# Layer hand-over in a DFT and attention kernel: transposes moved from after the last DFT stage into it, by four row tiles, with the small norm operations on GpSimd

## The chip, the cores and the metric

The kernel runs on one core of one Trainium2 chip. The metric is the time of one execution on the device in microseconds (us), the median of several executions. "Before" is the kernel before the change and "after" the kernel with it. Engines are named as the profile names them: PE is TensorE (matmuls and transposes), PEld its weight loads, DVE is VectorE, ACT is ScalarE, POOL is GpSimd. PSUM is the on-chip memory into which TensorE writes its results here, SBUF the one from which the engines take their inputs; the copies bring results from PSUM to SBUF. The granted clock is the share of full speed that the chip allowed TensorE, as the profile records it.

## The reference

The model alternates two layers twice, each on a layer-normed input with a residual. Layer A is a two-dimensional DFT filter. Layer B is attention by segments of 32 tokens with 8 memory tokens that are handed from segment to segment.

```python
def _A_ref(x, w_r, w_i):
    X = rfft2(x.astype(float32)) * (w_r + 1j * w_i)
    return irfft2(X, s=(S, D)).astype(bfloat16)

def _B_ref(x, mem0, Wq, Wk, Wv, Wo, seg_len):
    mem = mem0
    for s in range(n_seg):                       # 64 segments of 32 tokens
        h = concatenate([mem, x[:, s*seg_len:(s+1)*seg_len]], axis=1)
        q, k, v = h @ Wq, h @ Wk, h @ Wv         # ... 32 heads of 128
        p = softmax(where(mask, q @ k.T * scale, -1e9))
        o = (p @ v) @ Wo
        mem = o[:, :M]; outs.append(o[:, M:])    # ...

x = x + _A_ref(_layernorm(x), A_w_r, A_w_i)      # x: 1 x 2048 x 640
x = x + _B_ref(_layernorm(x), ...)
x = x + _A_ref(_layernorm(x), A_w_r, A_w_i)
x = x + _B_ref(_layernorm(x), ...)
```

What matters here is the seam from A to B. It occurs twice. Layer B multiplies with the *transposed* normed tokens (`hT`; 640 channels as 5 blocks of 128 partitions), and layer A ends with tokens on the partitions, in 16 row tiles of 128 tokens.

## The kernel before

The last DFT stage works through the 16 row tiles. For each tile it makes two products: `psg` (channel DFT, copied to SBUF by ScalarE) and, one tile later, `psy` (token DFT plus residual, copied by ScalarE into `x`). VectorE takes the statistics of every tile and normalises every pair of tiles. `add_u` sums each segment's tokens with a small matmul into `psu`.

```python
def _ln_apply(nc, pool, mv, xin, xout, nt, eps_t, on_dve=False):
    # ... Ln and Exp on ScalarE give r0, then four small operations on 2 columns:
    nc.vector.scalar_tensor_tensor(out=t, in0=mv[:, :nt, 1], scalar=LN_EPS, in1=r0, op0=ALU.add, op1=ALU.mult)
    nc.vector.tensor_tensor(out=t, in0=t, in1=r0, op=ALU.mult)
    nc.vector.tensor_scalar(out=t, in0=t, scalar1=-0.5, scalar2=1.5, op0=ALU.mult, op1=ALU.add)
    nc.vector.tensor_tensor(out=t, in0=t, in1=r0, op=ALU.mult)
    if on_dve:
        for t in range(nt):
            nc.vector.tensor_scalar(out=xout[:, t, :], in0=xin[:, t, :], scalar1=mv[:, t, 0:1], scalar2=rs[:, t:t + 1], op0=ALU.subtract, op1=ALU.mult)
    # ...

# the stage, in layer A's tokens():
for s0 in range(16 + 5):
    if s0 < 16:
        spectrum_d(s0)                    # 6 matmuls -> psg, ScalarE copy (L399)
    if 1 <= s0 <= 16:
        tokens(s0 - 1)                    # 6 matmuls -> psy, ScalarE copy into x, statistics
    if s0 >= 2 and s0 % 2 == 1 and s0 < 18:
        norm((s0 - 3) // 2)               # _ln_apply of two tiles into xna
    if handoff is not None:
        # ...
        if s0 >= 5:
            handoff.add_u(pp, xna[:, s0 - 5, :], s0 - 5)
if handoff is not None:
    handoff.finish(pp)                    # psu -> u
pp.release()
if handoff is not None:
    handoff.transpose_all(xna)
```

The hand-over stands after the stage. For each of the five channel blocks it makes 16 transposes into one PSUM tile and empties that by groups of 15 segments, in runs of 16 neighbouring keys:

```python
def transpose_all(self, xna):
    # ...
    for c in range(5):
        ps = pt.tile([128, 16, 128], BF16, name="pstr", tag="pstr")
        for s0 in range(16):
            nc.tensor.transpose(out=ps[:, s0, :], in_=xna[:, s0, c * 128:(c + 1) * 128], identity=ident[:])
        for g_ in range(4):
            b = st.kbase(g_ * GS)
            dst = hT[:, c, b:b + GS * SW].rearrange("p (w t) -> p w t", t=SW)[:, :, 1:SW].rearrange("p w (j s) -> p w j s", s=16)
            src = ps[:, :, 2 * GS * g_:2 * GS * (g_ + 1)].rearrange("p s (w j) -> p w j s", j=2)
            (nc.vector.tensor_copy if g_ % 2 == 0 else nc.scalar.copy)(out=dst, in_=src)
        # ... four small copies for the last four segments
```

After that layer B starts with `psvb` (160 matmuls of the first guess of the memories), then its long loop over heads.

## Time and profile before

| | before |
|---|---|
| time, median of 4 runs (range) | 1655.17 us (1654.39 to 1655.83) |
| window: first matmul of the last DFT stage to first `psvb`, layers 1 and 2 | 49.9 and 49.9 us |
| of it in layer 2: to the end of the last token matmul / from there to the end of the last norm / from there to `psvb` | 28.5 / 5.9 / 15.5 us |

I call the stretch from the first matmul of the last DFT stage to the first `psvb` matmul **the window**. It exists twice per execution.

TensorE is busy for 94% of the span, so a change of order can win time only where TensorE stands still. The windows view of before (busy us of each engine in each stretch, number of instructions, then the granted TensorE clock) shows where in layer 2 that is:

```profile
core 0: us, PE busy (x) PEld busy (x) DVE busy (x) ACT busy (x) POOL busy (x), PEclk, DMA share, GB/s
...
906.00:936.00 30.00, 28.68 (x257) 20.58 (x256) 24.03 (x82) 24.07 (x46) 1.46 (x2) 1.00 0.88 316
936.00:943.00 7.00, 2.15 (x30) 1.77 (x31) 4.73 (x28) 1.32 (x5) 0.00 (x0) 0.71 0.95 293
943.00:956.00 13.00, 7.33 (x77) 6.99 (x75) 7.66 (x20) 6.54 (x20) 0.00 (x0) 0.76 0.27 75
```

The stage itself (906 to 936) is limited by TensorE at full clock. The tail behind it (936 to 956) has TensorE busy for less than half. The timeline of TensorE in before (start, duration, what, and in brackets the idle time before it with its releaser) shows the pace and the waits:

```profile
919.55 1.00 PE L399 MATMUL psg<-A2gt_S,A2UT_S 128*128 128x321 bf16 x6
...
921.35 1.00 PE L399 MATMUL psg<-A2gt_S,A2UT_S 128*128 128x321 bf16 x6
...
937.28 0.68 PE L1191 MATMUL psu<-sel,A2tok_S 128*128 128x64 bf16 x10 [2.20 <-DVE A2tok_S L120]
940.51 0.81 PE L1191 MATMUL psu<-sel,A2tok_S 128*128 128x64 bf16 x10 [2.55 <-DVE A2tok_S L120]
...
942.50 4.37 PE L1206 MATMUL pstr<-ident,A2tok_S 128*128 128x128 bf16 x48
...
956.32 6.20 PE L1248 MATMUL psvb<-u,B2wv_S 128*128 128x64 bf16 x160 [3.49 <-DVE B2hT_S L1218]
```

One row tile costs 1.80 us (919.55 to 921.35), with no wait. All waits are in the tail. The view of the transposes' PSUM tile in before gives the price of one block copy (minimum/median/maximum in ns) and, under "its engine sat idle before it", how long copies waited for a copy of the other engine:

```profile
L1211 DVE COPY B2hT_S<-pstr x10: 647/652/658, 944.4 to 954.2; 128x480 bf16<-128x480 bf16 x10
L1211 ACT COPY B2hT_S<-pstr x10: 562/562/562, 945.2 to 954.8; 128x480 bf16<-128x480 bf16 x10
...
  DVE B2hT_S L1211: 6.7, 5
```

ScalarE's and VectorE's copies out of one PSUM tile take turns; in before ScalarE stands idle for 6.7 us ahead of such copies, in the tail.

### The profile page before, as it was taken

Reading aid. Unit: us, or ns where it says so; the run is one execution under the profiler, and the core shown is the slowest. Engines: PE = TensorE matmul, PEld = TensorE weight load, DVE = VectorE, ACT = ScalarE, POOL = GpSimd, SP = SyncE. Lnnn points to the kernel's source line nnn. Section 1 sums busy time; section 2 is a strip of 40 time slices with the busy share of each in tenths; the row PEclk is TensorE's granted clock in tenths of the full one; section 3 lists DMA queues with packets and bytes.
Section 4 is the critical chain, followed back from the end, with each engine's and each line's share of the span. In section 5 each row is a group of like instructions: output and inputs, shape, how many; then the busy total and the mean of one; then the engine's idle time right before and its main releaser. Section 6 shows DMA issues by size and latency. Waiting matters only on the chain. (4 is left out here: it accounts for less than half of the span.)

```text
span 1658.3 us, 36195 instructions
## 1 busy us (share of the span) xinstructions
PE 1563.1 (94%) x14240; PEld 1081.0 (65%) x14241; DVE 790.0 (48%) x2300; ACT 835.6 (50%) x2528; POOL 282.4 (17%) x206
## 2 busy tenths in 40 slices
PE   4887999999999999899988789999999999999998
PEld 2566666666666666677755666666666666666775
DVE  5772455555545554543356724545545454544110
ACT  5373566666666666511114636666666666663000
POOL 0810112121211111100026002121211111111000
PEclk9998999999999999999999899999999999999999
DMA  4472143434434343633302703434344343436241
GB/s 155 156 274 72 53 148 132 155 117 148 136 138 144 130 154 127 233 125 96 96 13 88 260 2 110 160 116 150 132 142 137 133 156 127 140 130 226 68 127 54
DMA packets 167873, 218.05 MB, mean 131 GB/s; under 512 B 7374, under 2 KB 141836, under 8 KB 159756
## 3 DMA queue, kind: packets, MB, share of 16 engines
q1 hardware_dynamic: 167084, 213.34, 38.5%
q8 instruction: 113, 1.85, 0.4%
q0 software_dynamic: 608, 2.30, 0.4%
q14 instruction: 68, 0.56, 0.1%
HBM read 170.52 MB, written 45.09 MB: 130 GB/s over the span
## 5 line engine op out<-in xcount | busy, mean ns | idle before, releaser
L846 PEld LDWEIGHTS <-bB_S 128*128 128x128 bf16 x3180 | 260.2, 97 | 185.9 <-issue 6.6
L990 DVE TENSOR_TENSOR bB_S<-pso,bB_S 128x480 bf16<-128x480 f32 (+1 forms) x320 | 189.4, 592 | 266.3 <-PE pso L981 249.4
L925 ACT ACTIVATE bB_S<-pss 128x269 bf16<-128x269 f32 (+5 forms) x576 | 213.3, 385 | 191.7 <-PE pss L922 177.2
L1140 PE MATMUL psx<-Wo_sb,bB_S 128*128 128x320 bf16 x2048 | 288.2, 299 | 3.9 <-DMA bB_S<-oTx_d 3.9
L1140 PEld LDWEIGHTS <-bB_S 128*128 128x128 bf16 x2048 | 197.2, 98 | 80.5 <-DMA bB_S<-oTx_d 4.6
L905 DVE CAST bB_S<-psk 128x495 bf16<-128x495 f32 (+3 forms) x320 | 191.3, 598 | 115.0 <-PE psk L846 84.8
L950 POOL TENSOR_TENSOR bB_S<-bB_S,bB_S 128x634 f32<-128x634 f32 x64 | 99.2, 1550 | 820.9 <-ACT bB_S L946 809.9
L926 DVE TENSOR_TENSOR bB_S<-bB_S,maskf 128x269 bf16<-128x269 bf16 (+5 forms) x576 | 162.9, 287 | 152.9 <-ACT bB_S L925 149.2
L914 ACT CAST bB_S<-psv 128x512 bf16<-128x512 f32 (+1 forms) x288 | 160.5, 557 | 83.8 <-PE psv L912 83.4
L890 ACT ACTIVATE bB_S<-psq 128x480 bf16<-128x480 f32 x300 | 152.5, 508 | 97.9 <-PE psq L846 97.9
L846 PE MATMUL psk<-B2hT_S,bB_S 128*128 128x495 bf16 (+3 forms) x800 | 165.0, 342 | 2.6 <-DVE bB_S L905 1.4
L846 PE MATMUL psk<-B1hT_S,bB_S 128*128 128x495 bf16 (+3 forms) x800 | 165.0, 342 | 1.7 <-DVE B1hT_S L1225 1.2
L912 PE MATMUL psv<-bB_S,B1hT_S 128*128 128x256 bf16 x1360 | 163.4, 272 | 0.2 <-DVE bB_S L905 0.2
L912 PE MATMUL psv<-bB_S,B2hT_S 128*128 128x256 bf16 x1360 | 163.4, 272 | 0.2 <-DVE bB_S L905 0.2
L922 PEld LDWEIGHTS <-bB_S 128*128 128x128 bf16 x1216 | 103.1, 98 | 90.1 <-issue 6.3
L846 PE MATMUL psq<-B2hT_S,bB_S 128*128 128x495 bf16 (+5 forms) x780 | 157.6, 336 | 0.1
L846 PE MATMUL psq<-B1hT_S,bB_S 128*128 128x495 bf16 (+5 forms) x780 | 157.5, 336 | 0.1
L922 PE MATMUL pss<-bB_S 128*128 128x132 bf16 (+8 forms) x1216 | 148.4, 216 | 3.0
L912 PEld LDWEIGHTS <-B1hT_S 128*128 128x128 bf16 x1360 | 128.7, 98 | 13.7 <-issue 0.3
L912 PEld LDWEIGHTS <-B2hT_S 128*128 128x128 bf16 x1360 | 128.6, 98 | 13.7 <-issue 0.3
L981 PE MATMUL pso<-bB_S,bB_S 128*128 128x132 bf16 (+8 forms) x1216 | 119.6, 216 | 0.0
L981 PEld LDWEIGHTS <-bB_S 128*128 128x128 bf16 x1216 | 91.2, 98 | 15.7 <-DVE oTmf L991 0.5
(225 smaller groups left out, 1555.1 us busy)
## 6 DMA issues: line engine op xcount, KB each, us to landing
bB_S<-Rd SPq DMA_DIRECT2D x62, 1059.5 KB
oTx_d<-bB_S SPq DMA_DIRECT2D x60, 512.0 KB
bB_S<-oTx_d SPq DMA_DIRECT2D x56, 512.0 KB
bB_S<-in_B_Wq_dram SPq DMA_DIRECT2D x32, 320.0 KB
bB_S<-in_B_Wk_dram SPq DMA_DIRECT2D x32, 320.0 KB
bB_S<-in_B_Wv_dram SPq DMA_DIRECT2D x32, 320.0 KB
bB_S<-oTx_d SPq DMA_DIRECT2D x14, 384.0 KB
Wo_sb<-in_B_Wo_dram SPq DMA_DIRECT2D x4, 1280.0 KB
```

The source lines that it names most:

```text
L846: nc.tensor.matmul(ps, lhsT=w[:, ch, hh * 128:(hh + 1) * 128], rhs=src[:, ch, lo:hi], start=(ch == 0), stop=(ch == 4))
L890: nc.scalar.mul(out=qv[:, :, 0:SEG], in_=x_view(ps, o, n)[:, :, 1:SW], mul=scale)
L905: nc.vector.tensor_copy(out=KTs[h % 2][:, lo:hi], in_=ps[:, 0:hi - lo])
L912: nc.tensor.matmul(ps[:, i * 256:(i + 1) * 256], lhsT=hT[:, ch, (t + i) * 128:(t + i + 1) * 128], rhs=w["Wv"][:, ch, :], start=(ch == 0), ...
L914: nc.scalar.copy(out=V[:, t:t + n, :].rearrange("p a b -> p (a b)"), in_=ps[:, 0:n * 256])
L922: nc.tensor.matmul(ps[:, off - o0:off - o0 + hi - lo], lhsT=KT[:, t * 128:(t + 1) * 128], rhs=QT[:, lo:hi], start=True, stop=True)
L925: nc.scalar.activation(out=E[:, 0:n], in_=ps[:, 0:n], func=ACTF.Exp)
L926: nc.vector.tensor_tensor(out=P[:, o0:o0 + n], in0=E[:, 0:n], in1=bs.mask[:, o0:o0 + n], op=ALU.mult)
L950: nc.gpsimd.tensor_tensor(out=accS, in0=accS, in1=sums_sb, op=ALU.add)
L981: nc.tensor.matmul(pso[:, lo - q0:hi - q0], lhsT=V[:, t, (h % 2) * 128:(h % 2 + 1) * 128], rhs=P[:, off:off + hi - lo], start=(i == 0), st ...
L990: nc.vector.tensor_tensor(out=oT.rearrange("p (r s j) -> p r s j", r=16, j=2)[:, :, s0:s0 + ns, :], in0=byclass(po), in1=rx, op=ALU.mult)
L1140: self.tc.nc.tensor.matmul(ps[:, 0:320], lhsT=lhs(h, k // 2), rhs=self.g["Wo_sb"][:, h, c0:c0 + 320], start=(h == 0), stop=(h == H - 1))
```

## The change

Its intent is to empty the tail. Every four row tiles, the transposes of those tiles stand inside the stage, by two channel blocks per iteration, and only the last four tiles are left for the tail. Because a copy then sees four row tiles and not sixteen, it writes runs of four keys. To let one copy cover all four groups of segments, they get an equal pitch in `hT`, which shifts its columns from 512 on by 7. `norm` is split: the small operations go to GpSimd (`inverse`), the scaling stays on VectorE (`_ln_scale`) and comes one iteration later. The diff, cut to its core:

```diff
+def _ln_inverse(nc, pool, mv, nt, eps_t, small):
+    # ... Ln, Exp on ScalarE as before, then the small operations on `small`;
+    # GpSimd: five operations in place of VectorE's four
+        def inverse(q):
+            rs[q], _ = _ln_inverse(nc, wk, mv[q], 2, g["eps"], nc.gpsimd if q < 7 else nc.vector)
...
-            for s0 in range(16 + 5):
-                if s0 < 16:
-                    spectrum_d(s0)
-                if 1 <= s0 <= 16:
-                    tokens(s0 - 1)
-                if s0 >= 2 and s0 % 2 == 1 and s0 < 18:
-                    norm((s0 - 3) // 2)
-                    ...
-                    if s0 >= 5:
-                        handoff.add_u(pp, xna[:, s0 - 5, :], s0 - 5)
+            for i in range(16 + 4):
+                if i < 16:
+                    spectrum_d(i)
+                    ...
+                    if i >= 7 and i < 19 and (i - 7) % 4 < 3:
+                        handoff.rows(pp, xna, (i - 7) // 4, (i - 7) % 4 * 2)
+                    for s0 in range(i - 5, min(i - 4, 14)) if i < 19 else (14, 15):
+                        if s0 >= 0:
+                            handoff.add_u(pp, xna[:, s0, :], s0)
+                if 1 <= i <= 16:
+                    tokens(i - 1)
+                if i >= 3 and i % 2 == 1 and i < 18:
+                    inverse((i - 3) // 2)
+                if i >= 4 and i % 2 == 0 and i < 19:
+                    norm((i - 4) // 2)
+            if handoff is not None:
+                handoff.finish(pp)
+                handoff.rows(pp, xna, 3, 0, big=True)
+                handoff.rows(pp, xna, 3, 4)
...
+    def hcol(self, k):
+        return k + (self.PRE if k >= 512 else 0)          # PRE is 7
...
+    def rows(self, pp, xna, q, c0, big=False):
+        c1 = min(5, c0 + (4 if big else 2))               # channel blocks c0 to c1 of row tiles 4q to 4q+3
+        # ... one PSUM tile: "pstr" (one buffer), or a big one for four channel blocks
+        for c in range(c0, c1):
+            for i in range(4):
+                nc.tensor.transpose(out=ps[:, c - c0, i, :], in_=xna[:, s0 + i, c * 128:(c + 1) * 128], identity=self.g["ident"][:])
+        for c in range(c0, c1):
+            v = grp[:, c, :, :]...                        # all four groups of 15 segments
+            (nc.vector.tensor_copy if c % 2 == 0 else nc.scalar.copy)(
+                out=v[:, :, :, :, s0:s0 + 4], in_=ps[:, c - c0, :, 0:120].rearrange("p s (g w j) -> p g w j s", g=4, j=2))
+        for j in range(2):                                # the last four segments
+            nc.scalar.copy(out=v[:, :, :, j, s0:s0 + 4], in_=ps[:, 0:c1 - c0, :, 120 + j:120 + 2 * n:2].rearrange("p c s w -> p c w s"))
```

More of the change, by code (lines that the diff above doesn't have):

```diff
@@ L105, in _ln_stats @@
     nc.vector.bn_aggr(out=mv[:, t, :], in_=st[:, t, :, :])
-def _ln_apply(nc, pool, mv, xin, xout, nt, eps_t, on_dve=False):
+def _ln_inverse(nc, pool, mv, nt, eps_t, small):
     rs = pool.tile([128, 4], FP32, name="lnrs", tag="lnrs")
@@ L113, in _ln_apply, with _ln_scale @@
     nc.scalar.activation(out=r0, in_=r0, func=ACTF.Exp, scale=-0.5)
-    nc.vector.scalar_tensor_tensor(out=t, in0=mv[:, :nt, 1], scalar=LN_EPS, in1=r0, op0=ALU.add, op1=ALU.mult)
-    nc.vector.tensor_tensor(out=t, in0=t, in1=r0, op=ALU.mult)
-    nc.vector.tensor_scalar(out=t, in0=t, scalar1=-0.5, scalar2=1.5, op0=ALU.mult, op1=ALU.add)
-    nc.vector.tensor_tensor(out=t, in0=t, in1=r0, op=ALU.mult)
+    if small is nc.vector:
+        small.scalar_tensor_tensor(out=t, in0=mv[:, :nt, 1], scalar=LN_EPS, in1=r0, op0=ALU.add, op1=ALU.mult)
+    else:
+        small.tensor_scalar_add(out=t, in0=mv[:, :nt, 1], scalar1=LN_EPS)
+        small.tensor_tensor(out=t, in0=t, in1=r0, op=ALU.mult)
+    small.tensor_tensor(out=t, in0=t, in1=r0, op=ALU.mult)
+    small.tensor_scalar(out=t, in0=t, scalar1=-0.5, scalar2=1.5, op0=ALU.mult, op1=ALU.add)
+    small.tensor_tensor(out=t, in0=t, in1=r0, op=ALU.mult)
+    return rs, nb
+def _ln_scale(nc, mv, rs, xin, xout, nt):
+    for t in range(nt):
+        nc.vector.tensor_scalar(out=xout[:, t, :], in0=xin[:, t, :], scalar1=mv[:, t, 0:1], scalar2=rs[:, t:t + 1], op0=ALU.subtract, op1=ALU.mult)
+def _ln_apply(nc, pool, mv, xin, xout, nt, eps_t, on_dve=False):
+    rs, nb = _ln_inverse(nc, pool, mv, nt, eps_t, nc.vector)
     if on_dve:
-        for t in range(nt):
-            nc.vector.tensor_scalar(out=xout[:, t, :], in0=xin[:, t, :], scalar1=mv[:, t, 0:1], scalar2=rs[:, t:t + 1], op0=ALU.subtract, op1=ALU.mult)
+        _ln_scale(nc, mv, rs, xin, xout, nt)
         return
@@ L128, in _ln_tiles @@
     st = pool.tile([128, 4, 2, nc.vector.BN_STATS_DIM], FP32, name="lnst", tag="lnst")
-    mv = pool.tile([128, 4, nc.vector.BN_AGGR_DIM], FP32, name="lnmv", tag="lnmv")
+    mv = pool.tile([128, 4, nc.vector.BN_AGGR_DIM], FP32, name="lnmv", tag="lnmv", bufs=3)
     return st, mv
-SLOT = dict(S1=20480, S2=10880, S3=12288, S4=10240, S5=12166, S6=11776)
+SLOT = dict(S1=20480, S2=10940, S3=12288, S4=10240, S5=12166, S6=11776)
 class _Cut:
@@ L417, in tokens @@
                 nc.sync.dma_start(out=xd[:, 2 * q:2 * q + 2, :], in_=x[:, 2 * q:2 * q + 2, :])
+        rs = {}
+        def inverse(q):
+            rs[q], _ = _ln_inverse(nc, wk, mv[q], 2, g["eps"], nc.gpsimd if q < 7 else nc.vector)
         def norm(q):
             xno = xna[:, 2 * q:2 * q + 2, :]
-            _ln_apply(nc, wk, mv[q], x[:, 2 * q:2 * q + 2, :], xno, 2, g["eps"], on_dve=True)
+            _ln_scale(nc, mv[q], rs[q], x[:, 2 * q:2 * q + 2, :], xno, 2)
             nc.sync.dma_start(out=xnd[:, 2 * q:2 * q + 2, :], in_=xno)
         with tc.manual_schedule(engines={nc.tensor.engine, nc.scalar.engine, nc.vector.engine}):
-            for s0 in range(16 + 5):
-                if s0 < 16:
-                    spectrum_d(s0)
-                if 1 <= s0 <= 16:
-                    tokens(s0 - 1)
-                if s0 >= 2 and s0 % 2 == 1 and s0 < 18:
-                    norm((s0 - 3) // 2)
-                if handoff is not None:
-                    if s0 < 10:
-                        handoff.wv_piece(s0)
-                    if s0 >= 5:
-                        handoff.add_u(pp, xna[:, s0 - 5, :], s0 - 5)
-        if handoff is not None:
-            handoff.finish(pp)
+            for i in range(16 + 4):
+                if i < 16:
+                    spectrum_d(i)
+                if handoff is not None:
+                    if i < 10:
+                        handoff.wv_piece(i)
+                    if i == 4:
+                        handoff.memory(pp)
+                    if i >= 7 and i < 19 and (i - 7) % 4 < 3:
[13 more added lines that the diff above has]
+                handoff.rows(pp, xna, 3, 4)
         pp.release()
-        if handoff is not None:
-            handoff.transpose_all(xna)
 H, DH, MEM, SEG, NSEG = 32, 128, 8, 32, 64
@@ L526, in __init__ @@
             qpos[b:b + SW] = np.concatenate([MEM + np.arange(SEG), [MEM - 1]])
+        self.hgap = [(self.hcol(a), self.hcol(b)) for a, b in ((502, 512), (1007, 1024), (1519, 1536), (2035, 2048))]
         self.q0 = [0] + [self.qbase(g * GS) for g in range(1, self.NG)] + [self.NQ]
@@ L844, in chain @@
         def chain(w, hh, ps, src, lo, hi):
+            if src is hT:
+                lo, hi = st.hcol(lo), st.hcol(lo) + hi - lo
             for ch in range(5):
@@ L861, in q_x @@
                 n = GS if g_ < NG - 1 else 3
-                b = st.kbase(g_ * GS)
+                b = st.hcol(st.kbase(g_ * GS))
                 ps = pj.tile([128, 512], FP32, name="psq", tag="pj")
@@ L911, in v_tiles @@
                 for ch in range(5):
-                    nc.tensor.matmul(ps[:, i * 256:(i + 1) * 256], lhsT=hT[:, ch, (t + i) * 128:(t + i + 1) * 128], rhs=w["Wv"][:, ch, :],
+                    nc.tensor.matmul(ps[:, i * 256:(i + 1) * 256], lhsT=hT[:, ch, st.hcol((t + i) * 128):st.hcol((t + i) * 128) + 128], rhs=w["Wv"][:, ch, :],
                                      start=(ch == 0), stop=(ch == 4))
@@ L1171, in begin @@
     def begin(self):
-        self.hT = self.ar.get("S2", f"{self.lname}hT").bf(5, self.st.NK)
-        for a, b in ((502, 512), (1007, 1024), (1519, 1536), (2035, 2048)):
+        self.hT = self.ar.get("S2", f"{self.lname}hT").bf(5, self.st.NK + 12)
+        for a, b in self.st.hgap:
             self.tc.nc.gpsimd.memset(self.hT[:, :, a:b], 0.0)
@@ L1192, in add_u @@
                              skip_group_check=True)
-    def transpose_all(self, xna):
-        nc, g, st, hT, tc = self.tc.nc, self.g, self.st, self.hT, self.tc
-        ident, SW, GS = g["ident"], st.SW, st.GS
-        with tc.tile_pool(name="bs_pt", bufs=3, space=PSUM) as pt, tc.tile_pool(name="bs_pm", bufs=1, space=PSUM) as pm:
-            psm = pm.tile([128, 5, MEM], BF16, name="psm0")
-            for c in range(5):
-                nc.tensor.transpose(out=psm[:, c, :], in_=self.m0[:, c * 128:(c + 1) * 128], identity=ident[:MEM, :MEM])
-            nc.vector.tensor_copy(out=hT[:, :, 0:MEM], in_=psm[:])
-            nc.vector.tensor_copy(out=self.gq[:, :, 0:1], in_=psm[:, :, MEM - 1:MEM])
-            for c in range(5):
-                ps = pt.tile([128, 16, 128], BF16, name="pstr", tag="pstr")
-                for s0 in range(16):
-                    nc.tensor.transpose(out=ps[:, s0, :], in_=xna[:, s0, c * 128:(c + 1) * 128], identity=ident[:])
-                for g_ in range(4):
-                    b = st.kbase(g_ * GS)
-                    dst = hT[:, c, b:b + GS * SW].rearrange("p (w t) -> p w t", t=SW)[:, :, 1:SW].rearrange("p w (j s) -> p w j s", s=16)
-                    src = ps[:, :, 2 * GS * g_:2 * GS * (g_ + 1)].rearrange("p s (w j) -> p w j s", j=2)
-                    (nc.vector.tensor_copy if g_ % 2 == 0 else nc.scalar.copy)(out=dst, in_=src)
-                b = st.kbase(4 * GS)
-                dst = hT[:, c, b:b + 3 * SW].rearrange("p (w t) -> p w t", t=SW)[:, :, 1:SW].rearrange("p w (j s) -> p w j s", s=16)
-                nc.vector.tensor_copy(out=dst, in_=ps[:, :, 120:126].rearrange("p s (w j) -> p w j s", j=2))
-                b = st.kbase(NSEG - 1) + 1
-                nc.scalar.copy(out=hT[:, c, b:b + 16], in_=ps[:, :, 126])
-                nc.scalar.copy(out=hT[:, c, b + 16:b + SEG - st.TAIL], in_=ps[:, 0:16 - st.TAIL, 127])
-                nc.vector.tensor_copy(out=hT[:, c, st.TAILK:st.TAILK + st.TAIL], in_=ps[:, 16 - st.TAIL:16, 127])
@@ new lines, in memory @@
+    def memory(self, pp):
+        nc = self.tc.nc
+        psm = pp.tile([128, 5, 128], BF16, name="psm0", tag="pstr")
+        for c in range(5):
+            nc.tensor.transpose(out=psm[:, c, 0:MEM], in_=self.m0[:, c * 128:(c + 1) * 128], identity=self.g["ident"][:MEM, :MEM])
+        nc.vector.tensor_copy(out=self.hT[:, :, 0:MEM], in_=psm[:, :, 0:MEM])
+        nc.vector.tensor_copy(out=self.gq[:, :, 0:1], in_=psm[:, :, MEM - 1:MEM])
+    def rows(self, pp, xna, q, c0, big=False):
+        nc, st, hT = self.tc.nc, self.st, self.hT
+        SW, GS, s0 = st.SW, st.GS, 4 * q
+        c1 = min(5, c0 + (4 if big else 2))
+        if big:
+            ps = pp.tile([128, 4, 4, 128], BF16, name="pstrb", tag="pg", bufs=3)
+        else:
+            ps = pp.tile([128, 2, 4, 128], BF16, name="pstr", tag="pstr")
+        n = 4 if q < 3 else 3
+        b = st.hcol(st.kbase(4 * GS))
+        win = hT[:, :, b:b + 4 * SW].rearrange("p c (w t) -> p c w t", t=SW)
+        grp = hT[:, :, st.PRE:st.PRE + 4 * 512].rearrange("p c (g k) -> p c g k", g=4)[:, :, :, 0:GS * SW]
+        for c in range(c0, c1):
+            for i in range(4):
+                nc.tensor.transpose(out=ps[:, c - c0, i, :], in_=xna[:, s0 + i, c * 128:(c + 1) * 128], identity=self.g["ident"][:])
+        for c in range(c0, c1):
+            v = grp[:, c, :, :].rearrange("p g (w t) -> p g w t", t=SW)[:, :, :, 1:SW].rearrange("p g w (j s) -> p g w j s", s=16)
+            (nc.vector.tensor_copy if c % 2 == 0 else nc.scalar.copy)(
+                out=v[:, :, :, :, s0:s0 + 4], in_=ps[:, c - c0, :, 0:120].rearrange("p s (g w j) -> p g w j s", g=4, j=2))
+        v = win[:, c0:c1, 0:n, 1:SW].rearrange("p c w (j s) -> p c w j s", s=16)
+        for j in range(2):
+            nc.scalar.copy(out=v[:, :, :, j, s0:s0 + 4], in_=ps[:, 0:c1 - c0, :, 120 + j:120 + 2 * n:2].rearrange("p c s w -> p c w s"))
+        if n == 3:
+            nc.scalar.copy(out=win[:, c0:c1, 3, 1 + s0:5 + s0], in_=ps[:, 0:c1 - c0, :, 126])
+            nc.scalar.copy(out=hT[:, c0:c1, st.hcol(st.TAILK):st.hcol(st.TAILK) + 4], in_=ps[:, 0:c1 - c0, :, 127])
@@ L1223, in scatter @@
             lo, hi = max(1, g_ * st.GS), min((g_ + 1) * st.GS, NSEG)
-            b = st.kbase(lo)
+            b = st.hcol(st.kbase(lo))
             nc.vector.tensor_copy(out=hT[:, :, b:b + (hi - lo - 1) * st.SW + 1:st.SW], in_=gq[:, :, lo:hi])
```

## The prediction

> **What bounds now.** TensorE: 94% busy, 41% of the span on the chain of waits. The change touches the last DFT stage and the transposes before layer B, twice per run (timeline: second 906 to 956 us).
>
> - Stage, 906.4 to 935: TensorE-bound, 1.80 us per row tile back to back (28.7 of 30 us busy, clock 1.00; ScalarE and VectorE 24 each).
> - Tail, 935 to 956.3: TensorE mostly waits. Last norm done 940.8; 80 transposes from 942.5; VectorE and ScalarE copies (652/562 ns, taking turns) until 956.2; then psvb starts. Clock 0.71 to 0.76.
> - First stage matmul to psvb: 49.9 us.
>
> **Removed from the tail.** 60 of 80 transposes and three quarters of the copies. After the last norm I expect 0.35 us psu, 20 transposes (1.5 us at low clock), then copies in turn c0 VectorE, c1 ScalarE, c2, c3 (4 x 0.65), eight small ScalarE copies (about 0.07 each): about 5.4 us against 15.5. Gain 10 us per layer.
>
> **Added inside the stage.** TensorE +3.4 us (60 x 56 ns, the trace's spacing at 128 columns); VectorE +9 copies x 0.6, minus 7 x 0.74 of small norm operations; ScalarE +6 copies x 0.46 and 18 small ones. As busy time it fits; the order does not:
>
> 1. psu and transposes now stand *before* the iteration's token matmuls, and norm moved half a pair later. So in every odd iteration TensorE waits: token matmuls end, x copy (0.2+0.7 us), statistics (1.05), the new norm's scale (0.4 to 0.8), against only 0.83 us of DFT matmuls to cover it. Stall about 1.7 us per pair. Before, slack was nearly two iterations.
> 2. ScalarE's block copy waits for VectorE's and precedes the x copy, which the next statistics await, which precede the next VectorE block copy. Loop: copy 0.7, copy+small 0.6, x copy 0.7, statistics 1.05, norm 0.7 every second: over 3 us against 2.2 of TensorE.
>
> Walking the queues in program order with these durations gives 45 us to the last token matmuls (before: 28.7 measured; the same walk 28.2), psvb at 55 to 56, or 58 if the clock sags to about 0.85 (it is 0.84 to 0.88 in the preceding spectrum stage). An estimate: net +6 to +8 us per layer, twice.
>
> GpSimd: the Trainium skill (GPSIMD Engine Reference, section 3.1) puts its two-input operations at about half VectorE's speed; from the trace's large ones (1.55 us for 634 columns) I estimate 0.3 us per small one. Below about 0.5 us they are off the chain.
>
> hT shifts 7 columns. The skill (SBUF, Operand start alignment) asks only element alignment; the trace agrees: q matmuls at odd columns take 372 ns, k ones from aligned columns 372. No effect elsewhere.
>
> **Predicted: 1668 us, 1652 to 1684 (8 in 10).** Faster by over 2%: 0.02; within 2%: 0.87; slower by over 2%: 0.11.
>
> **Right or wrong in the profile.** Stage to last token matmuls 40 to 50 us, with TensorE waiting on norm outputs before psu or transposes in odd iterations; ScalarE block copies waiting on VectorE ones; clock in the stage below 1.00; last norm to psvb 5 to 7 us; layer B's period unchanged.
>
> **What would make it wrong.** If the stage stays near 33 us (order harmless), about 1640. If small GpSimd operations take 0.7 us, norm waits for them: 4 to 8 us more per layer. If weight loads from the shifted hT slow (1360 psv matmuls per layer), far slower.

## More of the kernel before

Lines of the page of before. The first is the span, the second busy time per engine, then two groups of layer B's matmuls (busy us, mean ns of one | idle before them).

```profile
span 1658.3 us, 36195 instructions
...
PE 1563.1 (94%) x14240; PEld 1081.0 (65%) x14241; DVE 790.0 (48%) x2300; ACT 835.6 (50%) x2528; POOL 282.4 (17%) x206
...
L846 PE MATMUL psk<-B2hT_S,bB_S 128*128 128x495 bf16 (+3 forms) x800 | 165.0, 342 | 2.6 <-DVE bB_S L905 1.4
...
L846 PE MATMUL psq<-B2hT_S,bB_S 128*128 128x495 bf16 (+5 forms) x780 | 157.6, 336 | 0.1
```

## The result, and the profile after

After takes 1678.63 us (median of 4 runs, 1676.28 to 1681.61), before 1655.17 us. The ratio is 1.0143, with a 95% interval of 1.0125 to 1.016: 23.5 us or 1.4% more.

| | before | after |
|---|---|---|
| time, us | 1655.17 | 1678.63 |
| window, layers 1 and 2, us | 49.9, 49.9 | 60.3, 60.4 |
| layer 2: to the end of the last token matmul, us | 28.5 | 47.3 |
| then to the end of the last norm, us | 5.9 | 7.1 |
| then to `psvb`, us | 15.5 | 6.0 |

After the last norm 9.5 us were gained, about what was expected. But the stage took 18.8 us more, and the stretch from its end to the last norm 1.2 us more. The page of after, the same lines:

```profile
span 1676.5 us, 36233 instructions
...
PE 1566.0 (93%) x14240; PEld 1078.0 (64%) x14241; DVE 783.0 (47%) x2228; ACT 837.9 (50%) x2556; POOL 295.7 (18%) x276
...
L878 PE MATMUL psk<-B2hT_S,bB_S 128*128 128x495 bf16 (+3 forms) x800 | 165.6, 343 | 2.8 <-DVE bB_S L937 1.5
...
L878 PE MATMUL psq<-B2hT_S,bB_S 128*128 128x495 bf16 (+5 forms) x780 | 158.0, 336 | 0.1
```

Busy time per engine is almost as it was; nothing on this page tells where 18 us of span went. (The profiled execution of before took 1660.0 us and so 5 us more than its timed runs' median; its first window begins 2.3 us later than that of after. So the spans of the two pages differ by less than the times.) The windows view of after shows it:

```profile
core 0: us, PE busy (x) PEld busy (x) DVE busy (x) ACT busy (x) POOL busy (x), PEclk, DMA share, GB/s
...
940.00:946.00 6.00, 4.56 (x49) 3.28 (x47) 3.19 (x9) 3.39 (x9) 0.92 (x5) 1.00 0.28 109
946.00:952.00 6.00, 3.44 (x26) 2.20 (x24) 3.89 (x10) 3.02 (x9) 1.08 (x5) 0.85 0.20 78
...
964.00:970.00 6.00, 2.68 (x32) 2.40 (x33) 4.05 (x22) 1.19 (x6) 0.00 (x0) 0.50 1.04 308
```

In the middle of the stage TensorE is busy for 4.56 of 6 us (before: 28.68 of 30), and VectorE and ScalarE for little more than half. No engine is full: this is a chain of waits, not a lack of throughput. TensorE's timeline in after shows which:

```profile
940.17 1.00 PE L412 MATMUL psg<-A2gt_S,A2UT_S 128*128 128x321 bf16 x6
941.00 0.28 PE L1248 MATMUL pstr<-ident,A2tok_S 128*128 128x128 bf16 x2
942.59 0.81 PE L1248 MATMUL pstr<-ident,A2tok_S 128*128 128x128 bf16 x6 [1.31 <-DVE A2tok_S L127]
...
948.45 0.38 PE L1248 MATMUL pstr<-ident,A2tok_S 128*128 128x128 bf16 x4 [0.88 <-ACT B2hT_S L1255]
950.51 0.46 PE L1223 MATMUL psu<-sel,A2tok_S 128*128 128x64 bf16 x5 [1.68 <-DVE A2tok_S L127]
...
968.75 1.90 PE L1248 MATMUL pstrb<-ident,A2tok_S 128*128 128x128 bf16 x16
...
974.40 1.81 PE L1288 MATMUL psvb<-u,B2wv_S 128*128 128x64 bf16 x31 [3.34 <-ACT B2hT_S L1258]
```

At 941.00 TensorE transposes two row tiles of a group of four and then stands for 1.31 us, because the third and fourth are just being normalised (L127 is the scaling). At 950.51 the `psu` matmuls wait for a norm as well. Both stand *ahead* of the next token matmuls in TensorE's order, so these wait too although their own inputs are there. At 948.45 it is a PSUM buffer: `pstr` has one, and ScalarE's last small copy frees it.

The same stretch on VectorE in after:

```profile
942.14 0.75 DVE L127 TENSOR_SCALAR A2tok_S<-bB1x_S,lnmv,lnrs 128x640 bf16<-128x640 bf16 x2
943.44 0.76 DVE L1251 COPY B2hT_S<-pstr 128x480 bf16<-128x480 bf16 x1 [0.55 <-PE pstr L1248]
945.73 0.89 DVE L104 BATCH_NORM_STATS2 lnst<-bB1x_S 128x6 f32<-128x320 bf16 x2 [1.53 <-ACT bB1x_S L427]
...
946.77 0.71 DVE L1251 COPY B2hT_S<-pstr 128x480 bf16<-128x480 bf16 x1
```

And on ScalarE in after:

```profile
944.23 0.73 ACT L1251 COPY B2hT_S<-pstr 128x480 bf16<-128x480 bf16 x1 [2.34 <-DVE B2hT_S L1251]
944.82 0.29 ACT L1255 COPY B2hT_S<-pstr 128x32 bf16<-128x32 bf16 x2
944.97 0.72 ACT L427 CAST bB1x_S<-psy 128x640 bf16<-128x640 f32 x1
```

Read the two together as a loop: VectorE's block copy (943.44), ScalarE's block copy of the same PSUM tile (944.23), ScalarE's small copies (944.82), ScalarE's copy into `x` (944.97), VectorE's statistics of that tile (945.73), and VectorE's next block copy (946.77). Once round is 3.33 us for one row tile of TensorE's work. Over four tiles, 930.91 to 944.07, the stage takes 13.16 us where before takes 7.2. The waits table of after for 914 to 975 us sums it up (who <- whom: us in total, times, longest):

```profile
ACT B2hT_S L1251 <- DVE B2hT_S L1251: 12.4, 8, 2.4
...
PE psu L1223 <- DVE A2tok_S L127: 8.4, 5, 2.2
...
PE pstr L1248 <- ACT B2hT_S L1255: 4.3, 4, 1.7
PE pstr L1248 <- DVE A2tok_S L127: 4.0, 3, 1.4
...
DVE B2hT_S L1251 <- ACT B2hT_S L1251: 0.8, 1, 0.8
```

Last, the block copies themselves, in the view of `pstr` in after, are dearer than before, at the same number of elements:

```profile
L1251 DVE COPY B2hT_S<-pstr x10: 682/736/762, 930.3 to 972.9; 128x480 bf16<-128x480 bf16 x10
...
L1251 ACT COPY B2hT_S<-pstr x6: 733/760/763, 931.1 to 962.1; 128x480 bf16<-128x480 bf16 x6
```

### The profile page after: what moved, and what is told of

Its sections match the earlier page's. It is cut to its first block, busy times and chain, and to the rows that moved or that the text cites. A ratio compares the mean times of both kernels' runs of the same rounds, so it can differ in the third digit from the quotient of the medians.

```text
span 1676.5 us, 36233 instructions
## 1 busy us (share of the span) xinstructions
PE 1566.0 (93%) x14240; PEld 1078.0 (64%) x14241; DVE 783.0 (47%) x2228; ACT 837.9 (50%) x2556; POOL 295.7 (18%) x276
## 5 line engine op out<-in xcount | busy, mean ns | idle before, releaser
L878 PE MATMUL psk<-B2hT_S,bB_S 128*128 128x495 bf16 (+3 forms) x800 | 165.6, 343 | 2.8 <-DVE bB_S L937 1.5
L878 PE MATMUL psq<-B1hT_S,bB_S 128*128 128x495 bf16 (+5 forms) x780 | 158.0, 336 | 0.1
L878 PE MATMUL psq<-B2hT_S,bB_S 128*128 128x495 bf16 (+5 forms) x780 | 158.0, 336 | 0.1
```

The costliest lines, as they stand in the source:

```text
L878: nc.tensor.matmul(ps, lhsT=w[:, ch, hh * 128:(hh + 1) * 128], rhs=src[:, ch, lo:hi], start=(ch == 0), stop=(ch == 4))
```

## The experiments

The theory, A: the loss is one of *order*. (A1) `psu` and the transposes stand right behind the norm that feeds them and ahead of the next token matmuls. (A2) Each PSUM tile is emptied by two engines in turn, which ties ScalarE's queue to VectorE's. Rival B: the added work itself (60 transposes and 15 block copies inside the stage) is too much. Rival C: GpSimd's latency sits on the norm's path. The nine runs, all with correct results:

| run | time, us (range) | before, us | ratio (95%) | windows, us |
|---|---|---|---|---|
| e1_small_dve | 1683.85 (1681.37 to 1685.89) | 1656.39 | 1.0162 (1.0145 to 1.0179) | 64.9, 61.0 |
| e2_late | 1662.29 (1660.09 to 1664.53) | 1656.39 | 1.0034 (1.0017 to 1.0051) | 52.6, 52.7 |
| e3_one_engine | 1667.93 (1665.11 to 1669.45) | 1656.39 | 1.0064 (1.0047 to 1.008) | 52.6, 55.8 |
| e4_late_one | 1648.52 (1648.28 to 1649.66) | 1656.39 | 0.9955 (0.9938 to 0.9971) | 46.1, 46.1 |
| e5_before_runs4 | 1664.47 (1661.32 to 1665.92) | 1656.90 | 1.0052 (1.0035 to 1.0069) | 50.9, 51.3 |
| e6_tail_order | 1644.21 (1641.15 to 1648.59) | 1656.90 | 0.9935 (0.9916 to 0.9955) | 43.4, 43.4 |
| e7_tail_small_dve | 1643.78 (1642.47 to 1644.86) | 1656.90 | 0.9921 (0.9905 to 0.9938) | 44.0, 44.0 |
| e8_tail_back | 1671.89 (1670.71 to 1672.75) | 1654.25 | 1.0104 (1.0088 to 1.0119) | 58.0, 56.8 |
| e9_shift_only | 1656.86 (1654.44 to 1658.31) | 1654.25 | 1.0012 (0.9998 to 1.0025) | 49.8, 49.6 |

By the record's line of 2% all of these, and the change itself, count as the same as before; the differences below are told by the intervals. After was not in the rounds of these runs. Where a run is compared with after I quote the two medians; taken from each run's own before, the steps are 4.0 us (e1), 17.6 (e2), 11.9 (e3) and 31.3 (e4).

### e1: the small operations back on VectorE

```diff
-            rs[q], _ = _ln_inverse(nc, wk, mv[q], 2, g["eps"], nc.gpsimd if q < 7 else nc.vector)
+            rs[q], _ = _ln_inverse(nc, wk, mv[q], 2, g["eps"], nc.vector)
```

> Undoes one part: the small norm operations of all eight pairs go back to VectorE, everything else as in the change. If GpSimd's latency is what costs (rival: five operations of about 0.28 us from start to start), this run is clearly faster than the change, 1665 us or less. By the theory (issue order) GpSimd sits off the chain with about 1 us to spare, and moving the operations back puts 0.7 us more into VectorE's queue in each of seven pairs, inside the ScalarE-VectorE loop: 1681 to 1687 us, first stage matmul to psvb about 2 us longer than the change's 60.4.

Measured: 1683.85 us, 5.2 us more than after. It is not faster, so rival C falls. In this order the move to GpSimd seems to help, by 4 to 5 us, though the intervals of the two ratios overlap and the windows grew unevenly, by 4.6 and 0.6 us; the first has two more stretches of half clock inside the stage than that of after, the second one fewer. The clearest sign that the small operations lengthen VectorE's part of the loop is a single tile at full clock in both: 5.58 us in e1 (938.07 to 943.65) against 4.90 in after (933.33 to 938.23). In the trace of after, GpSimd's four later small operations take 0.19 to 0.20 us each at 0.28 us from start to start, and the group that ends at 940.87 is done 1.27 us before the scaling at 942.14 that uses it.

### e2: users one iteration later

The transposes and `add_u` move back by one iteration, so that a norm has more than one tile of TensorE work between itself and its first user.

```diff
-                    if i >= 7 and i < 19 and (i - 7) % 4 < 3:
-                        handoff.rows(pp, xna, (i - 7) // 4, (i - 7) % 4 * 2)
-                    for s0 in range(i - 5, min(i - 4, 14)) if i < 19 else (14, 15):
+                    if i >= 8 and i < 19 and (i - 8) % 4 < 3:
+                        handoff.rows(pp, xna, (i - 8) // 4, (i - 8) % 4 * 2)
+                    for s0 in range(i - 6, i - 5) if i < 19 else (13, 14, 15):
```

> Same operations as the change, but psu and the transposes are issued one row tile later, so that TensorE has a whole iteration between a norm and its first use. Theory: the waits of TensorE for the normalized rows (13.7 us of TensorE waiting in the second stage, those before psu and transposes on VectorE's scale operations about 12.4 of it) mostly vanish, the ScalarE-VectorE alternation stays: first stage matmul to psvb about 6 us shorter (54), total about 1665 to 1668. Rival (the added work itself, the copies in runs of four keys and 3.4 us of transposes, fills the stage): work unchanged, so 1677 to 1680.

Measured: 1662.29 us, 16.3 us less than after, with the same operations. The result went past the theory's range on the good side. The waits table of e2 for 906 to 960 us:

```profile
ACT B2hT_S L1251 <- DVE B2hT_S L1251: 12.3, 8, 2.5
...
PE pstr L1248 <- DVE A2tok_S L127: 1.8, 2, 1.5
...
PE psu L1223 <- DVE A2tok_S L127: 1.0, 1, 1.0
```

TensorE's waits for the norm have shrunk from 8.4 to 1.0 us ahead of `psu` and from 4.0 to 1.8 us ahead of the transposes, and A2's wait of ScalarE for VectorE stands unchanged at 12.3 us. So A1 is shown, and it is one of two.

### e3: each PSUM tile emptied by one engine

Only the assignment of copies changes: VectorE empties the tile of channel blocks 2 and 3, ScalarE those of 0 and 1 and of 4, small copies with them.

```diff
+        copy = nc.vector.tensor_copy if c0 == 2 else nc.scalar.copy
...
-            (nc.vector.tensor_copy if c % 2 == 0 else nc.scalar.copy)(
-                out=v[:, :, :, :, s0:s0 + 4], in_=...)
+            copy(out=v[:, :, :, :, s0:s0 + 4], in_=...)
...
-            nc.scalar.copy(out=v[:, :, :, j, s0:s0 + 4], in_=...)
+            copy(out=v[:, :, :, j, s0:s0 + 4], in_=...)
...
+                handoff.rows(pp, xna, 3, 2, big=True)     # the tail's tile of four blocks becomes two of two
```

> Same order and the same copies as the change, but each PSUM tile with its two channel blocks is emptied by one engine alone (ScalarE, VectorE, ScalarE), so that ScalarE never waits for a VectorE copy. Theory: the ScalarE waits for VectorE copies (12.4 + 6.4 us in the second stage) go, TensorE still waits for norms: first stage matmul to psvb about 5 us shorter (55 to 56), total about 1667 to 1670. Rival (work itself): unchanged within 2 us or slower, since ScalarE gets 3 more block copies.

Measured: 1667.93 us, 10.7 us less than after. The waits table of e3 for 900 to 970 us:

```profile
ACT B2hT_S L1253 <- PE pstr L1250: 6.9, 6, 1.6
...
PE psu L1224 <- DVE A2tok_S L127: 4.9, 5, 1.2
...
PE pstr L1250 <- DVE A2tok_S L127: 4.0, 3, 1.4
```

ScalarE's wait for VectorE's copy of the same tile has left the waits table (ScalarE's block copies now wait for the transposes, 6.9 us), and TensorE's waits for the norm are still there (4.9 us ahead of `psu`, 4.0 us ahead of the transposes). So A2 is shown as well. Its two windows differ by 3.3 us: the stage of the second has two stretches of 3.4 us at a granted clock of 0.50 (from 928.7 and from 942.4), the stage of the first has none.

Why did they take turns? The Trainium skill's page "PSUM — Partial Sum Buffer", section "PSUM bank collisions raise a hardware error", says that two engines must not access the same bank and group of 32 partitions at once, reads by ScalarE and VectorE included, and that the compiler's scheduler adds a dependency between two such instructions. The traces fit it: the wait is 12.4 us in 8 waits where two engines share a tile, 6.7 us in 5 in before, and gone where one engine has the tile. Writing into `hT` together is not the reason: in the tail of e3 VectorE's block copy at 960.01 and ScalarE's at 959.78, out of different tiles, overlap. But a dependency set for each tile, whatever the bank, would give the same waits: in the tail of after VectorE's copy of block 2 waits for ScalarE's copy of block 1 (0.8 us, the last line of the waits table above) in a tile twice as large as `pstr`. No run tells the two reasons apart.

### e4: both

The edit is e2's and e3's together:

```diff
-                    if i >= 7 and i < 19 and (i - 7) % 4 < 3:
+                    if i >= 8 and i < 19 and (i - 8) % 4 < 3:
...
+        copy = nc.vector.tensor_copy if c0 == 2 else nc.scalar.copy
...
```

> Both edits together, the same work as the change. Theory: both loops gone, TensorE paces the stage at about 2.1 us per row tile, and the shorter tail is kept: first stage matmul to psvb 44 to 48 us against 49.9 before, total 1645 to 1653, a little faster than the kernel before. Rival (work itself): about 1675, far slower than before.

Measured: 1648.52 us, 30.1 us less than after and 7.9 us less than before (0.9955, the interval leaves out 1). The transposes and copies inside the stage are the same number as in after, so rival B falls: with this order the work costs less in the stage than it cost in the tail.

One part of my expectation missed. I had expected a period of four row tiles of 8.4 us. TensorE's timeline of e4 has 10.2:

```profile
912.25 0.61 PE L1250 MATMUL pstr<-ident,A2tok_S 128*128 128x128 bf16 x8
...
918.62 0.40 PE L1250 MATMUL pstr<-ident,A2tok_S 128*128 128x128 bf16 x4 [1.45 <-DVE B2hT_S L1256]
...
922.45 0.61 PE L1250 MATMUL pstr<-ident,A2tok_S 128*128 128x128 bf16 x8
```

Once in four tiles the transposes of channel block 4 wait 1.45 us for VectorE to empty the one `pstr` buffer. It shows what would be next in the stage, and I did not try it.

### e5: before with the new copies only

To price the four-key runs by themselves, before keeps its loop and its tail, and only its block copies take the new shape (with the shift of `hT` that this needs). Number of copies and elements stay.

```diff
-                for g_ in range(4):
-                    b = st.kbase(g_ * GS)
-                    dst = hT[:, c, b:b + GS * SW]...                      # one group, 16 keys in a run
-                    src = ps[:, :, 2 * GS * g_:2 * GS * (g_ + 1)]...
-                    (nc.vector.tensor_copy if g_ % 2 == 0 else nc.scalar.copy)(out=dst, in_=src)
+                for q in range(4):                                        # all groups, 4 keys in a run
+                    (nc.vector.tensor_copy if q % 2 == 0 else nc.scalar.copy)(
+                        out=v[:, :, :, :, 4 * q:4 * q + 4], in_=ps[:, 4 * q:4 * q + 4, 0:120].rearrange("p s (g w j) -> p g w j s", g=4, j=2))
```

> The kernel before, everything in its old place and order; only the shape of the block copies changes: still four copies of 480 columns per channel block, VectorE and ScalarE in turn, but each takes four row tiles of all four groups (runs of four keys) instead of sixteen row tiles of one group; hT is shifted by 7 columns as in the change. If the shape alone makes the copies dearer (they took 652 and 562 ns before, 736 and 760 ns in the change), they take the latter here too; 10 of each per layer, largely in turn, so first stage matmul to psvb 2 to 3 us longer (52 to 53) and 1659 to 1662 us in all. If instead the load of the running stage made them dearer, they stay at 650 and 560 ns and the time is that of before within 2 us. In either case layer B's period shows whether the shift of hT costs anything; I expect not.

The view of `pstr` in e5:

```profile
L1216 DVE COPY B2hT_S<-pstr x10: 704/740/768, 943.3 to 954.0; 128x480 bf16<-128x480 bf16 x10
L1216 ACT COPY B2hT_S<-pstr x10: 732/760/772, 944.1 to 954.8; 128x480 bf16<-128x480 bf16 x10
```

The shape takes the copy from 652 to 740 ns on VectorE and from 562 to 760 ns on ScalarE, the numbers of after. The shift is not the reason, for in e9, with the shift and the old copies, they take 650 and 560 ns. That part is shown for the shape as a whole: runs of four keys, and also four groups and a quarter of the tile in one copy; which of these costs was not tried. The rest missed my expectation: the windows grew by 1.0 and 1.3 us, not 2 to 3, and yet 1664.47 us is 7.6 us over before. The shift is worth about 2 us (e9), and some 3 us stay unexplained; the four runs spread over 4.6 us, and the profiled one, the fastest, is 4.4 us over before, which windows and shift account for.

### e6: the tail in a better order

On top of e4: at the end of the stage the last token matmuls go ahead of the third group's transposes, the last norm goes ahead of the copies that it does not need, and the third group's late copies all go to ScalarE.

```diff
+                if i == 16:
+                    tokens(15)
+                if i == 18:
+                    norm(7)
...
-                    if i >= 8 and i < 19 and (i - 8) % 4 < 3:
+                    if 8 <= i <= 16 and (i - 8) % 4 < 3:
...
+                handoff.rows(pp, xna, 2, 2, big=True)
+                handoff.rows(pp, xna, 2, 4, big=True)
+                handoff.add_u(pp, xna[:, 14, :], 14)
+                handoff.add_u(pp, xna[:, 15, :], 15)
...
-        copy = nc.vector.tensor_copy if c0 == 2 else nc.scalar.copy
+        copy = nc.vector.tensor_copy if c0 == 2 and s0 != 8 else nc.scalar.copy
```

> The last version with both edits, plus a tail in the order of its needs: the last token matmuls ahead of the third group's transposes, the last norm ahead of the copies that do not feed it, the third group's late copies on ScalarE. In the last version the last x copy stood 1.3 us behind ScalarE block copies and the last norm 1.4 us behind VectorE block copies. Theory: first stage matmul to psvb about 2.5 us shorter than the 46.1 of that version, so 43 to 44.5, total 1642 to 1646. If the tail is bound by something else (the low clock, psu, the release of PSUM), no gain: 1648.

Measured: 1644.21 us, windows of 43.4 us; 12.7 us less than before (0.9935). It beats both kernels. In layer 2 of the profiled execution, 1.5 of the 2.7 us gained on e4 lie ahead of the end of the last token matmul, 1.6 between it and the last norm, and 0.3 are lost after that.

### e7: e6 with the small operations on VectorE

The edit is e1's, on top of e6:

```diff
-            rs[q], _ = _ln_inverse(nc, wk, mv[q], 2, g["eps"], nc.gpsimd if q < 7 else nc.vector)
+            rs[q], _ = _ln_inverse(nc, wk, mv[q], 2, g["eps"], nc.vector)
```

> The same as the one before it, but the small norm operations on VectorE. If GpSimd's part is of use only where VectorE paces the stage, this is within 2 us of it, since with users a whole tile late VectorE has slack (it is busy about 25 of 34 us); if GpSimd's latency cost anything it is faster, and if VectorE was the limit it is 3 us or more slower. I expect 0 to +3 us.

Measured: 1643.78 us, the same as e6 within their ranges, with windows 0.6 us longer. In this order GpSimd neither helps nor hurts by more than that; in the change's order (e1) it was worth 4 to 5 us, part of which is the clock.

### e8: the change's order without its work

This is the sharpest test of A1 against B. The loop is that of after, GpSimd too, but no transpose and no block copy is in the stage; they are back in the tail as in before.

```diff
-                    if i >= 7 and i < 19 and (i - 7) % 4 < 3:
-                        handoff.rows(pp, xna, (i - 7) // 4, (i - 7) % 4 * 2)
...
-                handoff.rows(pp, xna, 3, 0, big=True)
-                handoff.rows(pp, xna, 3, 4)
         pp.release()
+        if handoff is not None:
+            handoff.transpose_all(xna)
```

> The loop order of the change (psu ahead of the token matmuls, norm half a pair later, small operations on GpSimd) with all 80 transposes and their copies back in the tail as before: the first of the two waits alone. Theory: each odd row tile from the fifth on holds TensorE about 1.6 us for a norm, six times, though no copy was added: first stage matmul to psvb about 8 us longer than before (57 to 59), total 1670 to 1674. Rival (added copies and transposes are the cost): no work is added to the stage, so it is as fast as before, 1654 to 1658.

Measured: 1671.89 us, 17.6 us over before, with no transpose or block copy added to the stage. The waits table of e8 for 905 to 965 us:

```profile
PE psu L1219 <- DVE A2tok_S L127: 11.6, 8, 2.3
```

The `psu` matmuls alone, about 0.3 us of TensorE per tile, stand still for 11.6 us when they come one norm too early. In TensorE's timeline six of these eight waits, 1.22 to 1.49 us each and 8.4 us together, lie inside the stage; the other two are in the tail, where before has such waits as well. 8.4 us is about what the windows of e8 are longer than those of before (8.1 and 6.9 us).

### e9: the shift of `hT` alone

Before, with only the 7 columns' shift (also a part of e5). Every place that reads or writes `hT` gets it:

```diff
+    def hcol(self, k):
+        return k + (self.PRE if k >= 512 else 0)
...
+            if src is hT:
+                lo, hi = st.hcol(lo), st.hcol(lo) + hi - lo
...
-                b = st.kbase(g_ * GS)
+                b = st.hcol(st.kbase(g_ * GS))
```

> A control: the kernel before with hT shifted by 7 columns from the second group on, nothing else (copies of sixteen-key runs). The run with four-key copies was 7 us slower than before in its rounds, of which its profile shows only about 2.3 us in the two tails. If the shift costs the rest, this is 3 to 5 us slower than before; if not, it is within 2 us of before. I expect within 2 us, as layer B's period did not change in any profile.

Measured: 1656.86 us against 1654.25 in five rounds, 1.0012 with an interval of 0.9998 to 1.0025: 2.6 us by the medians, a little over the 2 us that I expected, and the interval includes 1. The page of e9 nevertheless shows a steady trace of it in the groups of layer B:

```profile
L852 PE MATMUL psk<-B2hT_S,bB_S 128*128 128x495 bf16 (+3 forms) x800 | 165.6, 343 | 2.8 <-DVE bB_S L911 1.6
```

`psk` goes from 165.0 to 165.6 us, and `psq` from 157.6 to 158.0, which is about 1 us per layer. Every kernel with the shift that I looked at (after, e4, e5, e6, e9) shows the same numbers.

### Does the sum close?

| run | the two windows against before's, us | time against before's, us |
|---|---|---|
| after | +20.8 | +23.5 |
| e1 | +26.0 | +27.5 |
| e2 | +5.4 | +5.9 |
| e3 | +8.6 | +11.5 |
| e4 | -7.6 | -7.9 |
| e5 | +2.3 | +7.6 |
| e6 | -13.0 | -12.7 |
| e7 | -11.8 | -13.1 |
| e8 | +15.0 | +17.6 |
| e9 | -0.4 | +2.6 |

The windows come from one profiled execution each, the times from medians of several. Over all ten the times lie 1.7 us above the windows in the mean, about the worth of the shift, which all ten kernels have. So the windows carry the change. The largest remainder is e5's, 5.3 us, of which the shift is about 2.

## Why the prediction was right or wrong

The predicted time was 1668 us, 1652 to 1684; the measured one is 1678.6 us, within the range and 10.6 us above its middle. That it lies in the range says little, for the range was wide enough to hold the time of before too; the loss is 23.5 us where the middle meant 13. What carries weight is the mechanism, which the profile and the experiments bear out; sizes were off.

- **"What bounds now" was right.** TensorE bounds, the stage runs at 1.80 us per tile, and the tail is where TensorE waits.
- **Removed from the tail: right.** From last norm to `psvb` I predicted 5.4 us, measured 6.0; the gain of 10 us per layer was 9.5.
- **Point 1, the stall on the norm: right.** TensorE waits for L127 ahead of `psu` and the transposes, 12.4 us in 8 waits (8.4 and 4.0). Two of them, 3.9 us in all at 965.13 and 968.13, lie in the tail, where before has two of 4.8 us together; the other six are the stage's. The stall of "about 1.7 us per pair" is seen at 950.51 (1.68 us) and 942.59 (1.31 us). e2 (these waits shrink to 2.8 us and 16.3 us come back) and e8 (the order without the work costs 17.6 us) show it as a cause.
- **Point 2, the loop through both copy engines: right.** I predicted over 3 us per turn; it is 3.33 us once round and 3.29 us per tile over four (the second number holds the waits of point 1 as well). e3 shows it as a cause (10.7 us back), and e4 shows the two together account for more than the whole loss (30.1 us).
- **The sum of the walk was too small.** The step that failed is "45 us to the last token matmuls" and "psvb at 55 to 56, or 58 if the clock sags to about 0.85". Measured in layer 2: 47.3 to the end of the last one, and 60.4. (The 28.7 that the prediction gives for before runs to the end of the `psu` matmuls behind it; to the token matmul itself it is 28.5.) My terms sum to 55.5, and the 4.9 us over it split into 2.3 in the stage, 2.0 between last token matmul and last norm (7.1 against the 5.1 that my numbers imply), and 0.6 in the tail.
- **In the stage the mis-sized term was, as far as a sum can show it, the block copy.** I took its durations from before (0.65 us on VectorE, 0.56 on ScalarE), although the new copy has another shape. It costs 0.74 and 0.76 us. From start to start, the loop above has 0.79 us for VectorE's copy where I counted 0.7, and 0.74 us for ScalarE's copy with its small ones where I counted 0.6. As an estimate, nine times 0.09 and six times 0.14 are 1.7 us of the stage's 2.3. In the tail the four copies take 2.9 us (970.68 to 973.62, where the small ones begin) where I counted 2.6. e5 shows that the shape is the reason for the price; that the price is the reason for these 2 us rests on this sum, not on a run.
- **Between the last token matmul and the last norm** the walk left out a queue. The last norm's Ln on ScalarE (966.25) stands behind small copies that wait 2.51 us for VectorE's block copy, which itself stands behind the statistics. e3, in which these small copies no longer wait for VectorE, has 4.9 us from last token matmul to last norm, close to my 5.1; e2, which keeps waits of this kind, has 7.6.
- **The clock: half right.** I expected it below 1.00 in the stage. In layer 2 it was 1.00 until 950.15, 0.50 for the next 3.4 us, 1.00 again until 963.81, and 0.50 from there on through the tail, against means of 0.71 and 0.76 in before's tail. (The 0.85 above, for 946 to 952, is a mean of the two values.) The Trainium skill, "TensorE: Matmul & The Clock Gate", section "What's actually happening", says that after an idle window of about 3.4 us the array runs at half clock. The trace agrees on the half clock: the 16 transposes at 968.75 start 0.105 us apart (the next block follows at 970.43), those at full clock 0.056 us. It shows no idle window before it: in the 3.41 us ahead of 950.15 TensorE was busy for 1.21 us, in those ahead of 963.81 for 1.35 us. So here the half clock followed stretches in which stalls left TensorE busy for 35 to 40% of the time. The 16 transposes took 1.90 us where I had counted 1.5 for all 20 of the tail.
- **GpSimd: right.** I estimated 0.3 us per small operation and measured 0.28 from start to start. They are off the chain (e1 is not faster without them), and their worth is between nothing (e7) and 4 to 5 us (e1).
- **"hT shifts 7 columns ... no effect elsewhere" was slightly wrong.** It costs about 1 us per layer in busy time of `psk` and `psq`. My comparison of odd and aligned columns, both at 372 ns in before, did not compare like with like, and the page that I cited is about what is legal, not about speed: the odd ones (L865) have 480 columns in runs of 32, the aligned ones 495 in one run. By shape, in one layer, the 320 `psk` matmuls of 495 columns went from 75.9 to 76.2 us and the 300 `psq` ones from 70.5 to 70.7; the rest is in the other shapes.

## What to carry to other kernels

Work that is moved into a bound stage must fit into its *order* as well as into its busy time: count, for each instruction of the bounding engine, how much other work stands between its input's producer and itself, and keep a consumer a full tile of other work behind (e2). One engine per PSUM tile keeps the queues of the two copy engines independent, and the pair of both repairs was worth 30 us here where either alone left the kernel slower than it had been. When a copy changes its shape, take its duration from a copy of the new shape and not from the old one with the same number of elements.

## What the Trainium skill lacked or had wrong

- No page that I found prices a PSUM to SBUF copy by its access pattern. At 128x480 bf16, copies in runs of 16 elements within one group against runs of 4 over four groups took 652 against 740 ns on VectorE and 562 against 760 ns on ScalarE (medians, before and e5; run length and number of groups were not tried apart). It would belong to "VectorE: DVE Perf Modes" and "ScalarE: Activation LUTs".
- "SBUF — State Buffer", section "Operand start alignment", states what is legal and says of itself that it timed nothing. Here, the shift of a matmul operand by 7 bf16 columns took the two groups that read it from 165.0 to 165.6 us (800 matmuls) and from 157.6 to 158.0 us (780), as a small but steady price (e9).
- "GPSIMD Engine Reference", section 3.1, has no figure for tiny operations. Its factor of about two is for 2048 elements; two-column operations took 0.19 to 0.20 us on GpSimd (the first of each group 0.22 to 0.33) against 0.16 to 0.17 on VectorE, at 0.28 us from start to start on GpSimd and 0.20 on VectorE.
- "PSUM — Partial Sum Buffer", section "PSUM bank collisions raise a hardware error", tells the rule for correctness, but not what it does to a schedule: two engines emptying one tile in turn cost ScalarE 12.4 us of waiting in a 61 us window, and no wait of this kind once one engine had the tile.
